# Spectral block and token/channel mixer on one core: where one weight tile is narrowed, and what the later stages' transfers and differences stand behind

## The chip, the cores and the metric

One core of one Trainium2 chip runs the whole program. The metric is the device time of one execution in microseconds (us); lower is better. TensorE (PE) does the matrix products, VectorE (DVE), ScalarE (ACT) and GpSimd (POOL) do the elementwise work, SyncE (SP) only issues transfers; ACT issues some as well. A queue name with a q (SPq, ACTq) is that engine's transfer issues.

## The reference, cut to what matters

```python
# x: (8, 3008, 256); w_r, w_i: (256, 256); w_tok1: (3008, 256); w_tok2: (256, 3008); w_ch1: (256, 1536); w_ch2: (1536, 256)
X = np.fft.rfft(x, axis=1)
Yr = Xr @ w_r - Xi @ w_i + b_r
Yi = Xr @ w_i + Xi @ w_r + b_i
Y  = soft_threshold(Yr, 0.01) + 1j * soft_threshold(Yi, 0.01)
x  = np.fft.irfft(Y, n=3008, axis=1)
h  = relu(x.T @ w_tok1) @ w_tok2      # over tokens
u  = x + h.T
return u + relu(u @ w_ch1) @ w_ch2    # over channels
```

The weights of the mixer arrive as 64-bit floats and are narrowed to 32 bits on the chip.

## The kernel before, in words

The transform over 3008 points is split as 47 x 64. Each product is made of three passes of a high and a low part (`mm3`, lines 223 to 225: high weight by high data, by low data, low weight by high data), so most operands exist as a pair: `xh`/`xl`, `hh`/`hlo`, `w2h`/`w2l`. The low part is made by `split`: ACT casts the high part (L158), DVE or POOL subtracts it (L161).

The eight batches are worked on in units, `UNITS = [[0], [1], [2, 3], [4, 5], [6, 7]]`. `begin` does unit 0 and the loads and narrowing of the weights. `spectral` is a generator for unit 1 and the three pairs. One of its steps `n` runs a forward product (`px`, L531), the complex mixing (`pm`), the inverse (`pi`) and the product with `w_tok1` (`gp`). Between them DVE makes `xtl` (L540) and `xs` (L541) out of `px`, and `z` (L576, L577: bias and sum; L583, L584: threshold) out of `pm`; POOL makes `yl` and some `xtl`. After the last step of a unit `gh` and `gl`, the relu of `gp`, are written to memory as `g_d` (L634 to L639).

The next units' first stage runs beside these steps as jobs (`beside`): `load` (x, from SP), `total` (the sum of the two halves of x on POOL, L277, and their difference on DVE, L278, both into `sd`), `divide` (`xh` on ACT, L673, and two `xl` on DVE, L676), `product` (`p`, L223 to L225, then `a` by ACT and a write of `a_d`). The table `when` says at which step a job is due; `sd` has one buffer.

Unit 0's channel mixing, in narrow chunks, is the other stream: `channel(n)` makes `u` (`pu`), then for each of twelve `f` a product `ph` with `w_ch1`, the pair `hh` (ACT, L1063) and `hlo` (DVE, L1064), and two steps later `po` with `w_ch2` (`second`). A loop at the end of the program takes steps of both streams in turn, by estimated times (the numbers that the generators yield). Behind the last narrow chunk `channel7`, the wide chunks of all other units, fills the rest of the span; it needs the weight sums that `weigh` and `weigh2` (L1159 to L1179) make in the last narrow chunk.

A scheduler gives each engine its order. `tc.issue_after(ins)` adds one rule to it: what is issued inside stands behind `ins` on `ins`'s own engine. Nothing waits for a semaphore because of it.

`w_ch2` comes in six tiles r0 to r5 of 128 x 512 values. Narrowing one takes two ACT passes (L187, L189) and six DVE passes (L192 to L197); `narrow_steps` (L168) gives the same work in two halves. Before, r0 and r1 are narrowed in `begin`, r2 to r5 in chunk 0 at `f` = 0, 2, 4, 6, and split one `f` later:

```python
                if f in late:
                    split_w2(*late.pop(f))
                if f % 2 == 0 and f // 2 + 2 < NF // 2:
                    late[f + 1] = f // 2 + 2, narrow_w2(f // 2 + 2)
```

Of the kernel before, what the change touches and what calls it, by code (L numbers as in the profile page):

```python
# [137 lines left out]
def tile_kernel(ctx: ExitStack, tc: tile.TileContext, io):  # L138
# [254 lines left out]
    def make_w(kp, aw, pool):  # L393
# [5 lines left out]
        wf = pool.tile([128, 2, DT], F32, name="wf", bufs=4) if kp < KP - 2 else wk.tile([128, 2, DT], F32, tag="xtl", name="wf", bufs=2)  # L399
# [63 lines left out]
    def narrow_w2(r, pool=None):  # L463
        return load_wide(io["moe_w_ch2"][r], 512, pool)
# [16 lines left out]
    def parts(u):  # L481
# [6 lines left out]
        def load_unit(g):  # L488
            src = io["x"][bs[0] // 2, g].rearrange("q i (b c) -> q i b c", b=2)
            if nb == 2:  # L490
                x = wc["wk2"].tile([120, 2, nb, C], F32, name="x", bufs=2)
            elif not plain:
# [8 lines left out]
            DMA.dma_start(out=x, in_=src[:, :, bs[0] % 2:bs[0] % 2 + nb])  # L501
# [116 lines left out]
        def close():  # L618
# [5 lines left out]
            elif u == len(UNITS) - 1:  # L624
                gs = [t4([128, 2, w], n) for n in ("gh", "gl")]
                gs = [[g.bitcast(F32R)[:, j] for j in range(2)] for g in gs]
            elif nb == 1:
                gs = [wc["wk2"].tile([128, CW], F32R, tag=n, name="g", bufs=3) for n in ("hh", "hlo")]
                gs = [[g[:, j * w:(j + 1) * w] for j in range(2)] for g in gs]
            else:  # L630
                gs = [[wc["wk2"].tile([128, CW], F32R, tag=n, name="g", bufs=3) for _ in range(2)] for n in ("hh", "hlo")]
# [54 lines left out]
    def spectral():  # L686
# [34 lines left out]
        for j in range(2):  # L721
            job("load", j)
        yield "wait"
        for q in range(2):
            load_ws(q)
        job("divide", 0)
# [5 lines left out]
        for n in range(len(flat) + LAG + 2):  # L732
# [22 lines left out]
            if 0 <= m < len(flat):  # L755
# [38 lines left out]
            if 0 <= m < len(flat) and kps[flat[m][0]][0] == 1:  # L794
# [4 lines left out]
                sts[o] = split_w(wf, G), split_e(ef, V)  # L799
# [797 lines left out]
```

## Time and profile before

| what | us |
|---|---|
| median of three runs | 2295.73 |
| the runs | 2295.45, 2301.96, 2295.73 |
| the profiled execution | 2295.41 |
| its span, first to last instruction | 2293.5 |
| TensorE busy in the span | 2266.3 |
| VectorE busy | 1709.5 |
| ScalarE busy | 1478.6 |
| GpSimd busy | 1372.4 |

1.9 us of the profiled execution's time lie outside its span. The mean granted TensorE clock is 0.999. The profile is one execution: a timeline row gives the start, the duration, engine, line, operation, what is written from what, and in brackets how long the engine had been idle and for whom. A row of waits gives the sum, the number and the longest of them.

### The profile page before, as it was taken

How to read it: one execution, taken by the hardware profiler on the slowest of the kernel's cores; microseconds unless marked ns; L12 is line 12 of the kernel's file. 1: busy time of each engine (PE TensorE's matmuls, PEld its weight loads, DVE VectorE, ACT ScalarE, POOL GpSimd, SP SyncE). 2: the span in 40 equal slices, each digit the busy share in tenths (PEclk: the TensorE clock that was granted, in tenths of full speed). 3: DMA queues.
4: the chain of work that ended last, by engine and by line, in shares of the span. 5: the costliest groups of instructions: out<-in, count | busy, mean ns of one | idle time of the engine just before them, and what ended most of it. 6: DMA issues, size and time to landing. Idle time of an engine off the chain costs nothing.

```text
span 2293.5 us, 34800 instructions
## 1 busy us (share of the span) xinstructions
PE 2266.3 (99%) x12095; PEld 1972.1 (86%) x12095; DVE 1709.5 (75%) x2801; ACT 1478.6 (64%) x2703; POOL 1372.4 (60%) x1111
## 2 busy tenths in 40 slices
PE   8999999999999999999999999999999999999999
PEld 7879999989989988888988888898888889888887
DVE  7976776687886767777777787777778776777877
ACT  6765555465654445776676777667677766667775
POOL 0000233354553321887787888778788877878886
PEclk9999999999999999999999999999999999999999
DMA  8885566787876443112222211222221122222101
GB/s 231 254 255 170 147 203 214 237 270 249 258 229 229 165 152 106 49 54 70 85 62 70 65 53 51 70 85 62 70 65 47 58 70 85 63 70 65 51 9 37
DMA packets 150957, 277.22 MB, mean 121 GB/s; under 512 B 11077, under 2 KB 95389, under 8 KB 150781
## 3 DMA queue, kind: packets, MB, share of 16 engines
q1 hardware_dynamic: 115106, 208.21, 30.2%
q10 hardware_dynamic: 35675, 66.78, 8.7%
q8 instruction: 96, 1.57, 0.3%
q14 instruction: 80, 0.66, 0.1%
HBM read 177.57 MB, written 97.39 MB: 120 GB/s over the span
## 4 chain that ended last, share of the span: by engine, by line
PE 87%; DVE 6%; DMA 3%; issue 2%; ACT 1%; SPq 1%; POOL 1%; ACTq 0%; POOLq 0%; DVEq 0%
PE l L134 15%; PE sx L134 14%; PE sz L134 11%; PE sy L134 10%; PE sw L134 7%; PE px L531 3%; PE pm L223 2%; PE pm L225 2%; PE pm L224 2%; PE gp L225 1%; PE gp L223 1%; PE gp L224 1%; PE po L224 1%; PE po L225 1%; PE po L223 1%
## 5 line engine op out<-in xcount | busy, mean ns | idle before, releaser
L1281 POOL TENSOR_TENSOR op<-ts,op 128x512 fp32r<-128x512 f32 (+2 forms) x500 | 634.7, 1291 | 271.3 <-ACT op L1314 267.7
L1314 ACT ACTIVATE op<-ts 128x512 fp32r<-128x512 f32 (+2 forms) x500 | 308.8, 619 | 62.1 <-DVE ts L1284 46.6
L1281 DVE TENSOR_TENSOR uf<-sy,uf 128x512 f32<-128x512 f32 (+2 forms) x229 | 154.4, 674 | 216.7 <-PE sy L134 216.2
L134 PE MATMUL l<-op,ws 128*128 128x512 f32 (+2 forms) x1125 | 311.8, 385 | 0.0
L134 PEld LDWEIGHTS l<-op,ws 128*128 128x128 f32 x1125 | 211.2, 188 | 39.8
L1310 ACT ACTIVATE x<-sx 128x512 f32<-128x512 f32 (+2 forms) x252 | 148.7, 590 | 137.5 <-PE sx L134 136.8
L134 PE MATMUL sx<-ub,w 128*128 128x512 f32 (+2 forms) x756 | 211.0, 387 | 0.4 <-DVE ts L1284 0.4
L134 PE MATMUL sx<-ub,ws 128*128 128x512 f32 (+2 forms) x756 | 209.8, 386 | 0.0
L161 POOL TENSOR_TENSOR yl<-z,yh 128x512 fp32r<-128x512 f32 x72 | 96.2, 1336 | 126.6 <-ACT yh L158 120.8
L134 PEld LDWEIGHTS sx<-ub,w 128*128 128x128 f32 x756 | 141.5, 188 | 29.5 <-DVE ts L1284 2.1
L134 PEld LDWEIGHTS sx<-ub,ws 128*128 128x128 f32 x756 | 141.8, 188 | 27.0
L1281 POOL TENSOR_TENSOR op<-b,op 128x512 fp32r<-128x512 f32 (+2 forms) x125 | 159.6, 1276 | 0.6 <-ACT op L1314 0.2
L1281 DVE TENSOR_TENSOR x<-sw,x 128x512 f32<-128x512 f32 (+2 forms) x126 | 85.7, 680 | 93.1 <-PE sw L134 92.9
L277 POOL TENSOR_TENSOR sd<-x 120x512 f32<-120x512 f32 x39 | 61.7, 1581 | 149.0 <-ACT hh L1063 45.0
L223 PE MATMUL pm<-wmh,xth 128*128 128x256 f32 x504 | 145.3, 288 | 2.0 <-DVE z L577 2.0
L1334 ACT ACTIVATE x<-x 128x512 f32<-128x512 f32 (+2 forms) x125 | 78.0, 624 | 107.3 <-DVE x L1281 107.3
L225 PE MATMUL pm<-wmh,xtl 128*128 128x256 f32 x504 | 142.5, 283 | 0.0
L224 PE MATMUL pm<-wml,xth 128*128 128x256 f32 x504 | 142.4, 283 | 0.0
L134 PE MATMUL sy<-op,w2h 128*128 128x512 f32 (+2 forms) x458 | 140.2, 387 | 0.3 <-DVE uf L1281 0.3
L161 POOL TENSOR_TENSOR xtl<-xs,xth 128x256 fp32r<-128x256 f32 x84 | 68.1, 811 | 104.9 <-ACT xth L158 66.7
L161 POOL TENSOR_TENSOR wt<-aw,wt 128x512 fp32r<-128x512 f32 x12 | 16.3, 1360 | 180.6 <-ACT wt L158 180.6
L134 PEld LDWEIGHTS sz<-g,b 96*128 96x128 f32 x836 | 106.8, 191 | 2.7
(240 smaller groups left out, 6616.3 us busy)
## 6 DMA issues: line engine op xcount, KB each, us to landing
wt<-wt_d SPq DMA_DIRECT2D x28, 940.0 KB, 5.6
x<-in_x SPq DMA_DIRECT2D x39, 480.0 KB, 6.1
a<-a_d SPq DMA_DIRECT2D x36, 512.0 KB, 6.1
wt<-ws_d SPq DMA_DIRECT2D x36, 512.0 KB, 5.1
b_d<-bt ACTq DMA_DIRECT2D x36, 512.0 KB, 5.6
a_d<-a ACTq DMA_DIRECT2D x36, 480.0 KB, 4.2
wt<-wt_d SPq DMA_DIRECT2D x21, 752.0 KB, 5.0
b<-b_d SPq DMA_DIRECT2D x32, 480.0 KB, 6.2
```

The costliest lines, as they stand in the source:

```text
L134: return lambda *args, **kw: self.tc.keep_in_program_order(op(*args, **kw))
L161: lo_eng.tensor_tensor(out=lo, in0=src, in1=hi.bitcast(F32), op=ALU.subtract)
L223: PE.matmul(out, lhsT=wh, rhs=xh, start=start, stop=False, skip_group_check=more)
L224: PE.matmul(out, lhsT=wh, rhs=xl, start=False, stop=False, skip_group_check=more)
L225: PE.matmul(out, lhsT=wl, rhs=xh, start=False, stop=stop, skip_group_check=more)
L277: eng.tensor_tensor(out=sd[:, 0], in0=x[:, 0], in1=x[:, 1], op=ALU.add)
L531: PE.matmul(pt[:, o:o + 128], lhsT=x, rhs=f2cols(2 * kp + ab), start=True, stop=True)
L1281: eng.tensor_tensor(out=out, in0=in0, in1=in1, op=op)
L1310: pins[key] = S.activation(out=t, in_=src, func=func)
L1314: pins[k] = S.activation(out=ops[k][:, 0], in_=v[k] if src is None else src, func=AF.Copy if k[0] == "t" else AF.Relu)
L1334: pins["x2r"] = S.activation(out=v["x2"], in_=v["x2"], func=AF.Relu)
```

## The change

- `w_ch2`: the raw words of r0, r1 and r2 are loaded at `n == NC + 7` of `begin`, all three are narrowed and split there. r3 and r4 are loaded at the end of `begin`, r5 at `f == 5` of chunk 0; they are narrowed in halves at `f` = 0, 1 and 2, 3 and 8, 9, each half behind that step's `hh` and `hlo`.
- The write of the first `w_tok2` tile moves in the code from `begin` to `f == 2` of chunk 0.
- Unit 1's x: every third tile has a buffer of its own (tag `xtl`), two of them are issued earlier on SP. The pairs' first x, the first `aw` and `ef` tiles stand behind the last x of unit 1 (`wc["loaded"]`).
- In `spectral`, the next job's `total` and `divide` are issued together, both behind the mixing's `summed` (L577 before) and the total behind `xs`; before, a later job's total came one step earlier. The next x is loaded behind a job's product.
- The `g_d` writes: unit 1 two instead of four, the low one on SP; of the first two pairs the low parts on SP; the last pair two instead of four. `weigh` and `weigh2` stand behind `hlo`.

```diff
+    def steps_w2(r):
+        raw = load_raw(io["moe_w_ch2"][r], 512)
+        yield
+        tmp = wk.tile([128, 2, 512], F32, tag="o", name="wide", bufs=3)
+        steps = narrow_steps(raw, tmp[:, 0], tmp[:, 1])
+        next(steps)
+        yield
+        next(steps)
+        split_w2(r, tmp[:, 0])
+        yield
...
+            elif not plain and g % 3 == 0:
+                x = wk.tile([120, 2, nb, C], F32, tag="xtl", name="x", bufs=2)
...
-            DMA.dma_start(out=x, in_=src[:, :, bs[0] % 2:bs[0] % 2 + nb])
+            wc["loaded"] = DMA.dma_start(out=x, in_=src[:, :, bs[0] % 2:bs[0] % 2 + nb])
...
             if u:
-                for i in range(2):
-                    for j in range(2):
-                        PUT.dma_start(out=g_d[u][i, :, j * w:(j + 1) * w], in_=gs[i][j].bitcast(F32))
+                if nb == 1 or u == len(UNITS) - 1:
+                    gs = [[g] for g in whole]
+                for i, g in enumerate(gs):
+                    n = 2 * w // len(g)
+                    for j, part in enumerate(g):
+                        (DMA if i and u < len(UNITS) - 1 else PUT).dma_start(out=g_d[u][i, :, j * n:(j + 1) * n], in_=part.bitcast(F32))
...
-        for j in range(2):
-            job("load", j)
+        with tc.issue_after(wc["loaded"].ins):
+            for j in range(2):
+                job("load", j)
         yield "wait"
...
+        yield "rest"
+        with tc.issue_after(wc["hh"].ins), tc.issue_after(wc["hlo"].ins):
+            job("divide", 0)
...
+                ahead = when.get(n + 1)
+                with tc.issue_after(summed.ins), tc.issue_after(wc["xs"].ins):
+                    if ahead is not None:
+                        job("total", ahead)
                 with tc.issue_after(summed.ins):
-                    for ahead, what in ((when.get(n + 1), "divide"), (when.get(n + 2), "total")):
-                        if ahead is not None and jobs[ahead][0] > 2 and (what == "divide" or ahead > NG):
-                            job(what, ahead)
+                    if ahead is not None and jobs[ahead][0] > 2:
+                        job("divide", ahead)
...
-            ahead = when.get(n + 1)
-            if ahead is not None and jobs[ahead][0] > 2:
-                job("load", ahead + 2)
-            if j is not None and jobs[j][0] == 2:
+            if j is not None:
                 job("load", j + 2)
...
+                if n == NC + 7:
+                    f = [load_raw(io["moe_w_ch2"][r], 512, early) for r in range(3)]
                 if n == NC + 8:
                     split_wt2(0)
-                    keep_wt2(0)
+                    wc["wt2_0"] = wts[0]
                     done += extra(1)
-                if n in (NC + 9, NC + 10):
-                    f.append(narrow_w2(len(f), early))
+                if n in (NC + 9, NC + 10, NC + 11):
+                    f[n - NC - 9] = load_wide(None, 512, raw=f[n - NC - 9])
...
-        for r in range(2):
+        for r in range(3):
             split_w2(r, f[r])
+        for r in (3, 4):
+            w2s[r] = steps_w2(r)
+            next(w2s[r])
...
-                if f in late:
-                    split_w2(*late.pop(f))
-                if f % 2 == 0 and f // 2 + 2 < NF // 2:
-                    late[f + 1] = f // 2 + 2, narrow_w2(f // 2 + 2)
+                if f == 5:
+                    w2s[5] = steps_w2(5)
+                    next(w2s[5])
+                with tc.issue_after(wc["hh"].ins), tc.issue_after(wc["hlo"].ins):
+                    if f in (0, 1, 2, 3, 8, 9):
+                        next(w2s[{0: 3, 1: 3, 2: 4, 3: 4}.get(f, 5)])
...
                 if seven and f in SUMS:
-                    (weigh2 if SUMS.index(f) % 2 else weigh)(SUMS.index(f) // 2)
+                    with tc.issue_after(wc["hlo"].ins):
+                        (weigh2 if SUMS.index(f) % 2 else weigh)(SUMS.index(f) // 2)
```

What this does to the engines' orders is shown at three places (numbers behind a name tell its buffers apart). The first is DVE at the end of `begin`, where unit 1's third x tile is divided (its `xl` is made from `sd_1284` before, `sd_1294` now) and r2 is narrowed (`raw_1419` into `wide_1421` before, `raw_1148` into `wide_1237` now). Before:

```order
L161 TENSOR_TENSOR xl_1288<-sd_1275,xh_1287 120x512
L277 TENSOR_TENSOR sd_1313<-x_1282 120x256
L278 TENSOR_TENSOR sd_1313<-x_1282 120x256
L161 TENSOR_TENSOR et_2677<-ef_2144,et_2677 128x256
L193 TENSOR_SCALAR wide_1421<-raw_1419 128x512
L192 TENSOR_SCALAR wide_1421<-wide_1421 128x512
L194 SCALAR_TENSOR_TENSOR wide_1421<-wide_1421 128x512
L195 TENSOR_SCALAR wide_1421<-wide_1421 128x512
L161 TENSOR_TENSOR w2l_1331<-wide_1188,w2h_1330 128x512
L161 TENSOR_TENSOR xl_1317<-sd_1284,xh_1316 120x512
L161 TENSOR_TENSOR w2l_1331<-wide_1214,w2h_1330 128x512
L635 SCALAR_TENSOR_TENSOR gl_1306<-gp_1018,gh_1305 128x256
```

Now:

```order
L196 TENSOR_TENSOR wide_1237<-raw_1148,wide_1237 128x512
L277 TENSOR_TENSOR sd_1294<-x_1174 120x256
L197 TENSOR_TENSOR wide_1237<-wide_1237 128x512
L278 TENSOR_TENSOR sd_1294<-x_1174 120x256
L161 TENSOR_TENSOR xl_1298<-sd_1285,xh_1297 120x512
L277 TENSOR_TENSOR sd_1323<-x_1292 120x256
L278 TENSOR_TENSOR sd_1323<-x_1292 120x256
L161 TENSOR_TENSOR xl_1327<-sd_1294,xh_1326 120x512
L277 TENSOR_TENSOR sd_1344<-x_1321 120x256
L278 TENSOR_TENSOR sd_1344<-x_1321 120x256
L161 TENSOR_TENSOR w2l_1341<-wide_1191,w2h_1340 128x512
L645 SCALAR_TENSOR_TENSOR gl_1316<-gp_1018,gh_1315 128x256
```

r2's last pass (L197) now stands ahead of the second tile's `xl`, and the third tile's `xl` ahead of the first `w2l`; before, it stood behind four passes over r2 and a `w2l`.

The second is ACT at the end of unit 1, where `g` is written out (L639, now L652) while the first steps of the pairs run. Before:

```order
L538 COPY xs_4669<-px_4664 128x256
L639 DMA g_d1_95<-g_4648 128x256
L634 ACTIVATE g_4648<-gp_2990 128x256
L639 DMA g_d1_95<-g_4649 128x256
...
L539 CAST xth_4670<-px_4664 128x512
L673 CAST xh_4704<-sd_4609 120x1024
```

Now:

```order
L548 COPY xs_4664<-px_4659 128x256
L549 CAST xth_4665<-px_4659 128x512
L644 ACTIVATE g_4643<-gp_3010 128x256
L612 COPY bt_4708<-pi_4709 128x512
L652 DMA g_d1_95<-g_4643 128x512
L612 COPY bt_4708<-pi_4714 128x512
L158 CAST xth_4665<-xs_4664 128x256
```

`xth` stood behind four writes of `g` (the last two are left out) and stands ahead of the one that is left on ACT.

The third is DVE in the pairs, where a job's difference (`sd`, L278) and its two `xl` (L676, now L689) are made. Before, from one job's difference to its two `xl` in the next step:

```order
L278 TENSOR_TENSOR sd_4983<-x_4861 120x512
L583 TENSOR_SCALAR z_4976<-z_4976 128x512
L584 TENSOR_TENSOR z_4976<-z_4976 128x512
L540 TENSOR_TENSOR xtl_5017<-px_5010,xth_5016 128x512
L541 TENSOR_TENSOR xs_5015<-px_5010,xs_5015 128x256
L576 TENSOR_TENSOR z_5061<-pm_5042,bias_80 128x512
L577 TENSOR_TENSOR z_5061<-pm_5042,z_5061 128x512
L676 TENSOR_TENSOR xl_5070<-sd_4983,xh_5068 120x512
L583 TENSOR_SCALAR z_5061<-z_5061 128x512
L676 TENSOR_TENSOR xl_5071<-sd_4983,xh_5068 120x512
L584 TENSOR_TENSOR z_5061<-z_5061 128x512
L540 TENSOR_TENSOR xtl_5085<-px_5078,xth_5084 128x512
```

Now, the same of one job:

```order
L587 TENSOR_TENSOR z_5526<-pm_5507,z_5526 128x512
L278 TENSOR_TENSOR sd_5533<-x_5354 120x512
L593 TENSOR_SCALAR z_5526<-z_5526 128x512
L594 TENSOR_TENSOR z_5526<-z_5526 128x512
L550 TENSOR_TENSOR xtl_5561<-px_5554,xth_5560 128x512
L689 TENSOR_TENSOR xl_5538<-sd_5533,xh_5536 120x512
L689 TENSOR_TENSOR xl_5539<-sd_5533,xh_5536 120x512
L551 TENSOR_TENSOR xs_5559<-px_5554,xs_5559 128x256
```

The difference and the two `xl` of a job were a step apart, or the difference of the next job stood behind the `xl`, right ahead of `xtl`; now a job's three passes all stand between one step's `z` and the next `xs`. Of the order at the end of the narrow chunk one thing is used further on: on TensorE the 22 matmuls of the next `pu` and six of `ph` now stand ahead of the `po` that reads the third `hlo`; before, they stood behind it.

## Rows read from the trace of the kernel before

**Rows 1.** The page: the span, and TensorE's busy time.

```profile
span 2293.5 us, 34800 instructions
PE 2266.3 (99%) x12095; PEld 1972.1 (86%) x12095; DVE 1709.5 (75%) x2801; ACT 1478.6 (64%) x2703; POOL 1372.4 (60%) x1111
```

**Rows 2.** Busy time of each engine in the stretch that the change touches (columns: stretch, its length, busy us and count of PE, PEld, DVE, ACT, POOL, granted TensorE clock, share of the transfer engines, GB/s), the first and fourth of five stretches from 140 to 860 us, and their sum.

```profile
140.00:300.00 160.00, 156.02 (x927) 148.10 (x926) 118.08 (x213) 85.95 (x165) 23.20 (x18) 0.99 0.60 179
...
580.00:700.00 120.00, 118.45 (x767) 106.90 (x767) 99.94 (x159) 71.17 (x138) 61.72 (x51) 1.00 0.77 239
sum 720.00, PE 710.49 PEld 652.47 DVE 523.51 ACT 381.08 POOL 255.60; mean PE 142.10 PEld 130.49 DVE 104.70 ACT 76.22 POOL 51.12
```

**Rows 3.** What TensorE waited for between 140 and 900 us (sum, number of waits, longest).

```profile
PE po L224 <- DVE hlo L1064: 2.9, 4, 1.2
PE pm L223 <- DVE z L577: 2.0, 3, 1.0
PE p L223 <- DVE xs L541: 2.0, 2, 1.1
PE p L224 <- DVE xl L161: 1.5, 1, 1.5
PE pi L223 <- DVE xs L541: 0.9, 2, 0.4
PE p L223 <- ACT xh L158: 0.8, 1, 0.8
PE ph L223 <- DVE xs L541: 0.5, 1, 0.5
```

**Rows 4.** The chain of waits between 135 and 160 us (start, us, what): its two longest pieces of `w_ch2`.

```profile
134.45 6.61 DMA raw<-in_moe_w_ch
...
150.05 6.57 DMA raw<-in_moe_w_ch
```

**Rows 5.** DVE's timeline around the first of them: r2's first pass, and the `xl` behind the narrowing; then the pass over the next tile and the `hlo` behind it.

```profile
141.08 0.43 DVE L193 TENSOR_SCALAR wide<-raw 128x512 uint32<-128x512 uint32 x1 [4.07 <-DMA raw<-in_moe_w_ch]
...
143.93 0.68 DVE L161 TENSOR_TENSOR xl<-sd,xh 120x512 fp32r<-120x512 f32 x1
...
156.65 0.43 DVE L193 TENSOR_SCALAR wide<-raw 128x512 uint32<-128x512 uint32 x1 [2.45 <-DMA raw<-in_moe_w_ch]
156.99 1.20 DVE L1064 SCALAR_TENSOR_TENSOR hlo<-ph,hh 128x470 fp32r<-128x470 f32 x2
```

**Rows 6.** The same columns as rows 2, in stretches of 2 us behind the first stall; the granted clock is the third number from the end.

```profile
144.00:146.00 2.00, 1.33 (x8) 1.25 (x9) 2.00 (x6) 0.42 (x2) 0.00 (x0) 0.91 1.03 248
146.00:148.00 2.00, 2.00 (x7) 1.70 (x6) 1.56 (x4) 1.10 (x2) 0.29 (x1) 0.50 0.97 316
148.00:150.00 2.00, 2.00 (x14) 1.92 (x13) 2.00 (x4) 0.07 (x1) 1.41 (x1) 0.74 1.03 370
```

**Rows 7.** ACT's timeline at the end of unit 1: the writes of `g_d`, and the `xth` behind them.

```profile
454.24 0.78 ACTq L639 DMA_DIRECT2D g_d<-g  x1
...
455.09 3.11 ACTq L639 DMA_DIRECT2D g_d<-g  x3
458.24 0.59 ACT L539 CAST xth<-px 128x512 fp32r<-128x512 f32 x1 [2.79 <-DMA a_d<-a]
```

**Rows 8.** Transfers issued between 452 and 463 us: the four writes of `g_d` (size of one, median us from issue to landing).

```profile
g_d<-g ACTq DMA_DIRECT2D x4, 128.0 KB, 7.9
```

**Rows 9.** TensorE's timeline: the single stalls of rows 3 that the sum speaks of.

```profile
157.69 0.48 PE L224 MATMUL po<-hlo,w2h 128*128 128x470 f32 x1 [1.02 <-DVE hlo L1064]
...
441.22 0.47 PE L223 MATMUL p<-xh,f1r 120*128 120x512 f32 x1 [0.85 <-DVE xs L541]
...
460.09 0.47 PE L223 MATMUL p<-xh,f1r 120*128 120x512 f32 x1 [1.12 <-DVE xs L541]
461.41 0.36 PE L223 MATMUL pm<-wmh,xth 128*128 128x256 f32 x1 [0.85 <-DVE z L577]
...
506.98 0.47 PE L223 MATMUL pi<-yh,et 128*128 128x512 f32 x1 [0.45 <-DVE xs L541]
...
681.15 0.36 PE L223 MATMUL pm<-wmh,xth 128*128 128x256 f32 x1 [0.96 <-DVE z L577]
...
861.33 0.48 PE L224 MATMUL po<-hlo,w2h 128*128 128x470 f32 x1 [1.17 <-DVE hlo L1064]
```

**Rows 10.** DVE's timeline ahead of four of them: a difference ahead of 441, the first of eight that took 1.7 us and more between 421 and 686 us; a difference ahead of 507; the last of the eight and a weight sum ahead of 681; the `hlo` ahead of 861.

```profile
435.45 1.78 DVE L278 TENSOR_TENSOR sd<-x 120x512 f32<-120x512 f32 x1
...
504.12 1.78 DVE L278 TENSOR_TENSOR sd<-x 120x512 f32<-120x512 f32 x1
...
675.64 1.79 DVE L278 TENSOR_TENSOR sd<-x 120x512 f32<-120x512 f32 x1
...
678.28 1.39 DVE L1159 TENSOR_TENSOR a<-w 128x1024 f32<-128x1024 f32 x1
...
860.63 0.64 DVE L1064 SCALAR_TENSOR_TENSOR hlo<-ph,hh 128x470 fp32r<-128x470 f32 x1
```

**Rows 11.** All differences (L278) between 300 and 840 us: their number, the shortest, median and longest in ns.

```profile
L278 DVE TENSOR_TENSOR sd<-x x31: 678/798/1786, 311.1 to 685.3; 120x512 f32<-120x512 f32 x31
```

**Rows 12.** POOL's timeline: the sum that ran beside the difference of 435.45.

```profile
435.20 1.47 POOL L277 TENSOR_TENSOR sd<-x 120x512 f32<-120x512 f32 x1
```

**Rows 13.** What TensorE waited for ahead of 140 us: the one wait on narrowed weights of the first 64-bit matrix.

```profile
PE p L302 <- DVE wide L197: 0.6, 1, 0.6
```

More of the change, by code (lines that the diff above doesn't have):

```diff
@@ L398, in make_w @@
                 PE.matmul(pt[ab * 64:(ab + 1) * 64, i], lhsT=wc["fw"][:, i, j0:j0 + 64], rhs=aw[:, ab], start=True, stop=True)
-        wf = pool.tile([128, 2, DT], F32, name="wf", bufs=4) if kp < KP - 2 else wk.tile([128, 2, DT], F32, tag="xtl", name="wf", bufs=2)
+        wf = pool.tile([128, 2, DT], F32, name="wf", bufs=4) if kp < KP - 2 else wk.tile([128, 2, DT], F32, tag="xth", name="wf", bufs=2)
         for i in range(2):
@@ L624, in close @@
             elif u == len(UNITS) - 1:
-                gs = [t4([128, 2, w], n) for n in ("gh", "gl")]
-                gs = [[g.bitcast(F32R)[:, j] for j in range(2)] for g in gs]
+                whole = [t4([128, 2, w], n).rearrange("p j w -> p (j w)").bitcast(F32R) for n in ("gh", "gl")]
+                gs = [[g[:, j * w:(j + 1) * w] for j in range(2)] for g in whole]
             elif nb == 1:
-                gs = [wc["wk2"].tile([128, CW], F32R, tag=n, name="g", bufs=3) for n in ("hh", "hlo")]
-                gs = [[g[:, j * w:(j + 1) * w] for j in range(2)] for g in gs]
+                whole = [wc["wk2"].tile([128, CW], F32R, tag=n, name="g", bufs=3) for n in ("hh", "hlo")]
+                gs = [[g[:, j * w:(j + 1) * w] for j in range(2)] for g in whole]
             else:
@@ L719, in close @@
                 parts_of(kps[q][0]).close()
-        for j in range(2):
-            job("load", j)
+        with tc.issue_after(wc["loaded"].ins):
+            for j in range(2):
+                job("load", j)
         yield "wait"
-        for q in range(2):
-            load_ws(q)
-        job("divide", 0)
+        with tc.issue_after(wc["loaded"].ins):
+            for q in range(2):
+                load_ws(q)
+        yield "rest"
+        with tc.issue_after(wc["hh"].ins), tc.issue_after(wc["hlo"].ins):
+            job("divide", 0)
         job("load", 2)
@@ L798, in spectral @@
                     keep_split(o - 1, *sts[o - 1])
-                sts[o] = split_w(wf, G), split_e(ef, V)
+                with tc.issue_after(wc["hh"].ins):
+                    sts[o] = split_w(wf, G), split_e(ef, V)
                 if kps[o + 2][0] == 1:
@@ L815, in begin @@
         pieces = [(q, t) for q in range(3) for t in range(2)]
[L816 removed]
+        aws, wfs1, wide, done = {}, {}, {}, 0.0
         def transform(k):
@@ L949, in tile_kernel @@
     assert done_g == len(groups)
-    wts, wfs, b2s, ufs, us, late, mixed = {}, {}, {}, {}, {}, {}, {}
+    wts, wfs, b2s, ufs, us, late, mixed, w2s = {}, {}, {}, {}, {}, {}, {}, {}
     def load_wt2(g, pool=None, parts=(0, 1)):
@@ L973, in steps_wt2, with keep_wt2 @@
         return narrow_steps(raw, tmp[:, 0], tmp[:, 1])
-    def keep_wt2(g):
+    def keep_wt2(g, w=None):
         u, _, s, k = groups[g]
         if u == 0:
-            DMA.dma_start(out=wt2_d[:, :, s * TOKS:(s + k) * TOKS], in_=wts[g][:, :, :k * TOKS].bitcast(F32))
+            w = wts[g] if w is None else w
+            DMA.dma_start(out=wt2_d[:, :, s * TOKS:(s + k) * TOKS], in_=w[:, :, :k * TOKS].bitcast(F32))
     def split_wt2(g, parts=(0, 1)):
```

7 lines of the change are left out of this document (3 added, 4 removed).

## The prediction, before any run of the changed kernel

> **What bounds the kernel now.** I read the page first. TensorE is busy 2266.3 us of a span of 2293.5 [rows 1]: 27.2 us of idle time are all that a change of order can return, beside any time at the lower clock. The change touches what runs before 880 us; behind that TensorE's order is the same in both. So I asked for the busy time by stretch. From 140 to 860 us TensorE is busy 710.49 of 720 us [rows 2]: 9.5 us idle, 4.0 of them between 140 and 300. One more wait, 1.17 us, lies at 861 [rows 9]. Then I asked what TensorE waited for: by `hlo` 2.9 us in four waits, by `z` 2.0, by `xs` 2.0, 0.9 and 0.5, by `xl` 1.5, by `xh` 0.8 [rows 3], 10.6 us in all. Every one of them is a product that came late from DVE or ACT, while DVE as a whole has room: 99.94 of 120 us in its fullest stretch [rows 2]. So the order on DVE and ACT is what costs, not the sum of their work.
>
> The chain of waits tells why the first two stalls occur: the raw words of two tiles of `w_ch2`, issued at 134.45 and 150.05, take 6.61 and 6.57 us [rows 4]. DVE stands 4.07 us for the first, 2.45 for the second, and the `xl` and `hlo` that TensorE needs are queued behind [rows 5]. After the first stall the granted clock is 0.91, 0.50 and 0.74 of full speed in three stretches of 2 us [rows 6]; 0.50 is the lower level, 1.2 GHz, full speed is 2.4 GHz.
>
> **The change, part by part.** The sum is against the profiled execution, 2295.41 us, which is the span and 1.9 us around it; the median of the runs, 2295.73, is 0.3 us above it.
>
> A, r2 narrowed earlier. The two stalls are 0.8 and 1.5 us [rows 3]. The clock costs (0.09 + 0.50 + 0.26) x 2 = 1.7 us [rows 6]. Together 4.0. In the new order r2's raw words follow those of r0 and r1, and its last DVE pass is ahead of the second `xl`. The six passes that come in ahead need some 3 x 0.43 + 3 x 0.68 = 3.3 us, and the 4.07 us for which DVE stood [rows 5] cover them; without that cover `xl` would come 3.3 us later. What is late next is `gl`: one `w2l` stands ahead of its first half, a `w2l` and an `xl` ahead of its second, each 0.68 [rows 5]. SP's order also puts the raw words of r4 ahead of the `b` that `pu` needs; r4 waits for the third x tile's difference, an event some 3 us later than before, while `b` waits for a product that does not move. I take 0.4 us for what this leaves, between 0 and the 4.0 of the stall itself: gain 3.6.
>
> B, the `hlo` ahead of the narrowing. Three of the four `hlo` waits, 2.9 - 1.17 = 1.7 us [rows 3, 9], are in chunk 0 and the next: 1.02 at 157.69, the others shorter. The halves of r3 to r5 now stand behind `hh` and `hlo` of their step, and their raw words are asked for earlier. The work is the same, six DVE passes a tile; it is hidden as before. Gain 1.7, at least the 1.0.
>
> C, the writes of `g_d`. ACT issues four of them, 0.78 and 3.11 us, and `xth` starts 2.79 us late behind [rows 7]; TensorE waits 1.12 and 0.85 us at 460 [rows 9]. In the new order `xth` is ahead of the only write left on ACT; the other goes to SP, which has no engine behind it that waits so soon. Gain 2.0. The third `z` wait, 2.0 - 0.85 - 0.96 = 0.2 [rows 3, 9], is at the end of a pair behind the same kind of writes, two of which leave ACT: gain 0.2. The Trainium skill says that the engine which issues a transfer only saves its sequencer's time, "usually small relative to the DMA itself" (DMA: Bandwidth & Descriptors, section Issuing engines are not separate DMA queues). Here the issues took 3.9 us against 7.9 to landing [rows 7, 8], and it is ACT's time, not the transfer's, that `xth` waited for. By that sentence the sum would lose its 2.2 us of C; I go by the rows.
>
> D, a weight sum. 1.39 us of `weigh` run at 678.28, in the middle of the pairs [rows 10], and TensorE waits 0.96 [rows 9]. Behind `hlo` of its own chunk it moves to the end. Gain 1.0.
>
> E, the end of the narrow chunks. The third `hlo` starts at 860.63, behind passes of the weight sums [rows 10], and TensorE waits 1.17 [rows 9]. DVE's order there is worse now, by one weight sum as long as the 1.39 us of D, but TensorE has 28 other matmuls to do first: at a mean of 118.45 / 767 = 0.15 us [rows 2] these are 4.3 us, against 1.17 + 1.39. Gain 1.2, at worst none.
>
> F, the pairs. The waits by `xs` at 441.22 (0.85), the two of `pi` (0.9) and the one of `ph` (0.5) [rows 3, 9] are 2.25 us. Ahead of the two of which I show the DVE rows stands a difference of 1.78 us [rows 10]; the shortest takes 0.678 and the median is 0.798 [rows 11], so the long ones are stretched by 1.1 us, with POOL's sum beside them [rows 12]. In the new order no difference stands right ahead of `xtl`, which removes these waits. But now all three passes of a job stand between `z` and `xs`, 3 x 0.68 = 2.0 us, in each of the 31 jobs that rows 11 count. No row shows that in every job, so I bound it. A difference of 1.78 us in that place cost 0.45 where it cost most by itself [rows 9, 10]: 31 x 0.45 = 14.0 us above, and nothing below, since some steps hold two `xl` and a difference already. I take 0.11 each, the two `pi` waits spread over the eight stretched differences from 435.45 to 675.64 [rows 10], since in most of these eight places the delay cost nothing: 3.4 us. Net loss 1.15.
>
> G, the start. Two x tiles of unit 1 stand ahead of two tiles of `w_tok1` on SP. The nearest wait on narrowed `w_tok1` is 0.6 us [rows 13]; I take half, loss 0.3, between 0 and 0.6. The moved write of `w_tok2` costs nothing: on SP it stands between the same transfers as before.
>
> Sum: 3.6 + 1.7 + 2.2 + 1.0 + 1.2 - 1.15 - 0.3 = 8.25 us. 2295.41 - 8.25 = **2287.2 us**. 0.3%, 6.9 us, is about what a measurement of this kernel can tell from no change: 2288.5 is the bound against the profiled execution.
>
> **The rivals.**
> 1. The pairs give more back. If each job costs 0.25 us, 7.8 in place of 3.4, the time is 2291.6; for it speaks that DVE's load is high there [rows 2], against it that some steps held all three passes before. No change. Chance 0.24.
> 2. The change does not do what it says at the start: `b` comes late behind r4's raw words, `pu` waits as `p` did, and the clock falls again. A's 3.6 are gone: 2290.8. For it speaks that a raw tile took 6.6 us to land [rows 4]; against it that the pairs' x no longer compete there. No change. Chance 0.10.
> 3. Slower: DVE's three passes of a job meet POOL. A difference beside POOL's sum was stretched by 1.1 us [rows 10 to 12], and an `xl` also reads two tiles as a difference does. If all three are stretched in ten of the 31 jobs, about the third in which a difference is stretched now, `xs` comes 3.3 us later there; less the 0.65 us of slack that a stretched one leaves (1.1 late, 0.45 waited), that is 2.65 x 10 = 27 us; if one of the three is stretched in each job, 0.45 x 31 = 14. I price it in between, at 0.7 a job: without F's loss the gains are 11.65, and 2295.41 - 11.65 + 21.7 = 2305.5. It decides from 11.65 / 31 = 0.38 us a job on. Against it: POOL's sum still runs as soon as `sd` is free, while the difference now waits for the step, so these two should meet less often. Chance 0.12. The Trainium skill would have it so whenever both run: VectorE with two inputs from SBUF and a reading GpSimd take turns, and whichever starts first holds the other off for the whole instruction (SBUF — State Buffer, section Who interferes with whom). The stretched differences agree, 1.78 for 0.68.
> 4. C is not returned, since other work on ACT is as late: 2289.4, no change. Chance 0.04.
>
> **How the numbers follow.** The forecast has 0.50. The chance of faster by over 0.3% is that of the forecast, 0.50; within 0.3% are rivals 1, 2 and 4, 0.38; slower 0.12. The range begins at 2283.0, where every wait from 140 us on (10.6) and the clock's 1.7 come back, and ends at 2299.0: that takes in rivals 1, 2 and 4 with their bounds and the mild end of rival 3.
>
> **What would show it.** Right: no wait of `p` between 140 and 146 us and full clock to 152; `hlo` without a DMA wait ahead of it at 156; `xth` at the end of unit 1 directly behind `xs`; no weight sum before 840 us; TensorE busy over 717 of 720 us from 140 to 860. Wrong: a wait of `pu` on `b` with a clock of 0.5 near 145 (rival 2); many waits of `pm`, `p` or `pi` on `xs` or `z` between 300 and 700 us (rival 1), with `xl` and differences of 1.2 us and more (rival 3); the wait of `po` at 861 back as one of `ph`.

## The result: slower by 0.6%, and the profile after

| | before | changed |
|---|---|---|
| median (five runs each, on one chip), us | 2295.85 | 2312.98 |
| lowest and highest run of the changed kernel, us | | 2310.67, 2313.97 |
| ratio to before | | 1.0062 [1.0047, 1.0076] |
| profiled execution, us | 2295.41 | 2310.67 |
| its span, us | 2293.5 | 2308.8 |

Ratios, here and below, compare the runs as a whole and are not the quotients of the medians (here 1.0075). Predicted were 2287.2 us and a range of 2283.0 to 2299.0. The time lies outside the range, on the other side of no change. The page of the changed kernel answers to [rows 1]:

```profile
span 2308.8 us, 34754 instructions
PE 2275.2 (99%) x12095; PEld 1969.5 (85%) x12095; DVE 1725.2 (75%) x2801; ACT 1479.5 (64%) x2703; POOL 1370.5 (59%) x1111
```

Busy TensorE rose by 8.9 us with the same 12095 matmuls and a full clock. In the profile a matmul of 512 columns lasts 0.39 us, and the next one may start 0.23 us behind it (three of `gp` start at 611.71, 611.93 and 612.16), so the first 0.16 us of a stall pass as busy: the stall of `p` at 617.76, shown further down, cost 1.11 us and 0.96 of them count as idle. So busy time is a poor measure of what was lost, and I count matmuls too. What TensorE waited for between 140 and 900 us, to be read against [rows 3] (sum, number, longest):

```profile
PE p L224 <- DVE xl L689: 3.9, 7, 1.0
PE pu L223 <- ACT wt L158: 2.6, 2, 1.5
PE p L223 <- DVE xs L551: 1.6, 2, 1.1
PE p L223 <- ACT xh L686: 1.6, 3, 0.7
PE ph L223 <- ACT a L304: 1.2, 1, 1.2
PE gp L223 <- DVE g L645: 0.9, 1, 0.9
...
PE pm L223 <- DVE z L587: 0.7, 2, 0.5
...
PE p L223 <- DVE hlo L1088: 0.3, 1, 0.3
```

The waits by `hlo`, all but 0.3 us, and by `z`, all but 0.7, are gone as forecast. Of those by `xs`, 1.6 us are left, and in their place stand `xl` and `xh` of the pairs' first-stage product `p`, and `wt`. The stretches of the changed kernel (columns as in [rows 2]):

```profile
140.00:260.00 120.00, 120.00 (x707) 114.20 (x706) 83.85 (x160) 64.90 (x125) 10.68 (x8) 1.00 0.57 168
260.00:440.00 180.00, 175.14 (x1085) 160.93 (x1084) 125.57 (x187) 91.55 (x174) 60.13 (x46) 1.00 0.67 210
440.00:700.00 260.00, 249.68 (x1578) 218.45 (x1578) 209.03 (x319) 143.86 (x277) 122.26 (x105) 1.00 0.78 241
```

and of the kernel before:

```profile
140.00:260.00 120.00, 116.02 (x671) 109.45 (x670) 87.27 (x162) 64.56 (x124) 10.50 (x8) 0.99 0.64 191
260.00:440.00 180.00, 179.50 (x1126) 168.10 (x1124) 122.38 (x191) 93.17 (x178) 57.18 (x46) 1.00 0.64 200
440.00:700.00 260.00, 255.19 (x1658) 230.54 (x1657) 207.64 (x336) 150.48 (x292) 131.25 (x109) 1.00 0.79 247
```

The first stretch now has no idle time and 36 matmuls more. The second has 41 fewer, the third 80 fewer. For a closer account I took the time from each matmul's start to the next and summed by how much it differs from the median of that shape of matmul in the kernel before; shorter times count against longer ones. This is **lost time** in the text below, in us. Time at the lower clock is in it: 1.7 of the 7.8 us of the kernel before, and of e8's 1.7 from 140 to 260 and 3.4 in the pairs.

| stretch, us | before | changed | e1 | e4 | e8 | e14 |
|---|---|---|---|---|---|---|
| 0 to 140 | 39.5 | 40.0 | 40.7 | 41.5 | 41.1 | 41.6 |
| 140 to 260 | 7.8 | 1.9 | 2.2 | 2.8 | 9.1 | 3.6 |
| 260 to 440 | 1.8 | 7.5 | 5.6 | 6.4 | 1.7 | 1.8 |
| 440 to 700 | 6.9 | 20.2 | 4.1 | 5.0 | 22.4 | 3.3 |
| 700 to 880 | 3.7 | 3.4 | 2.6 | 2.6 | 4.5 | 2.5 |
| 880 to the end | 12.6 | 14.7 | 13.8 | 12.8 | 14.0 | 13.8 |
| sum | 72.3 | 87.6 | 68.9 | 71.0 | 92.9 | 66.6 |

The sums of the first two differ by 15.3 us, as their spans do. The changed kernel gains 6.0 us from 140 to 260 and loses 5.7 in the next stretch and 13.3 in the pairs. (e1 to e14 are the experiments below.)

**One job of the pairs.** DVE in the changed kernel (start, us, what):

```profile
612.71 1.05 DVE L278 TENSOR_TENSOR sd<-x 120x512 f32<-120x512 f32 x1
...
614.74 0.68 DVE L550 TENSOR_TENSOR xtl<-px,xth 128x512 fp32r<-128x512 f32 x1
615.34 2.37 DVE L689 TENSOR_TENSOR xl<-sd,xh 120x512 fp32r<-120x512 f32 x2
617.63 0.41 DVE L551 TENSOR_TENSOR xs<-px,xs 128x256 f32<-128x256 f32 x1
```

ACT, POOL and TensorE beside it:

```profile
613.79 1.05 ACT L686 CAST xh<-sd 120x1024 fp32r<-120x1024 f32 x1 [0.91 <-DVE sd L278]
...
615.55 1.60 POOL L161 TENSOR_TENSOR yl<-z,yh 128x512 fp32r<-128x512 f32 x1 [2.34 <-ACT yh L158]
...
617.76 0.50 PE L224 MATMUL p<-xl,f1r 120*128 120x512 f32 x1 [0.96 <-DVE xl L689]
```

The difference, `xh`, the two `xl` and the `p` that reads them are now one chain. The second `xl` ends at 617.71 and `p` starts 0.05 us later, after 0.96 us of idle time. The job at the same place before: DVE, then TensorE's last `p` with `xl`.

```profile
608.15 0.68 DVE L278 TENSOR_TENSOR sd<-x 120x512 f32<-120x512 f32 x1
...
614.03 0.68 DVE L676 TENSOR_TENSOR xl<-sd,xh 120x512 fp32r<-120x512 f32 x1
...
618.19 0.39 PE L224 MATMUL p<-xl,f1r 120*128 120x512 f32 x1
```

The second `xl` was done at 614.71, 3.48 us ahead of its reader. Over the 23 jobs whose difference lies between 440 and 700 us that lead had a median of 2.0 us and a least value of 1.3; now the median is 0.06 and 13 of the 23 have no more. And from the rows of `xl` in that stretch (ns: shortest, median, longest; below them who waited, us and times), before and changed:

```profile
L676 DVE TENSOR_TENSOR xl<-sd,xh x48: 677/682/1165, 442.4 to 694.3; 120x512 fp32r<-120x512 f32 x48
...
who waited for it (us, times):
  POOL sd L277: 1.6, 1
```

```profile
L689 DVE TENSOR_TENSOR xl<-sd,xh x46: 675/686/1792, 446.0 to 697.0; 120x512 fp32r<-120x512 f32 x46
...
who waited for it (us, times):
  PEld p L224: 10.3, 18
  PE p L224: 3.9, 7
```

TensorE waited for no `xl` of the pairs before. Now its weight loads waited 18 times for one and its matmuls seven times.

### The profile page after: what moved, and what is told of

Same layout as the page of the kernel before. It is cut to its first block, busy times and chain, and to the rows that moved or that the text cites. A ratio compares the mean times of both kernels' runs of the same rounds, so it can differ in the third digit from the quotient of the medians.

```text
span 2308.8 us, 34754 instructions
## 1 busy us (share of the span) xinstructions
PE 2275.2 (99%) x12095; PEld 1969.5 (85%) x12095; DVE 1725.2 (75%) x2801; ACT 1479.5 (64%) x2703; POOL 1370.5 (59%) x1111
## 4 chain that ended last, share of the span: by engine, by line
PE 82%; DVE 10%; issue 2%; DMA 2%; ACT 2%; POOL 1%; SPq 1%; ACTq 0%; DVEq 0%; POOLq 0%
PE l L134 14%; PE sx L134 13%; PE sz L134 10%; PE sy L134 10%; PE sw L134 7%; PE px L541 2%; PE pm L223 2%; PE pm L225 2%; PE pm L224 2%; PE gp L224 1%; PE gp L225 1%; PE gp L223 1%; PE ph L223 1%; PE po L223 1%; PE po L225 1%
## 5 line engine op out<-in xcount | busy, mean ns | idle before, releaser
L277 POOL TENSOR_TENSOR sd<-x 120x512 f32<-120x512 f32 x39 | 52.2, 1338 | 261.1 <-DMA aw<-w_d 155.5
L1310 DVE TENSOR_TENSOR x<-sw,x 128x512 f32<-128x512 f32 (+2 forms) x126 | 85.7, 680 | 92.9 <-PE sw L134 92.9
L134 PE MATMUL sw<-ub,ws 128*128 128x512 f32 (+2 forms) x378 | 107.6, 393 | 1.7 <-DVE op L1313 1.3
```

Source lines behind the costliest of these rows:

```text
L134: return lambda *args, **kw: self.tc.keep_in_program_order(op(*args, **kw))
L277: eng.tensor_tensor(out=sd[:, 0], in0=x[:, 0], in1=x[:, 1], op=ALU.add)
L1310: eng.tensor_tensor(out=out, in0=in0, in1=in1, op=op)
```

## The experiments

My theory: the total one step later (F) costs the pairs 13 us (20.2 for 6.9 in the table) and the start another 8, while A to E are returned. The rivals: the late load of x does it, or DVE's load by itself. Each ratio is to runs of the kernel before made beside it; e4, e8, e11 and e13 ran on another chip than the other experiments.

**e1, the order of the jobs put back in the changed kernel**, all else kept.

```diff
-                ahead = when.get(n + 1)
-                with tc.issue_after(summed.ins), tc.issue_after(wc["xs"].ins):
-                    if ahead is not None:
-                        job("total", ahead)
                 with tc.issue_after(summed.ins):
-                    if ahead is not None and jobs[ahead][0] > 2:
-                        job("divide", ahead)
+                    for ahead, what in ((when.get(n + 1), "divide"), (when.get(n + 2), "total")):
+                        if ahead is not None and jobs[ahead][0] > 2 and (what == "divide" or ahead > NG):
+                            job(what, ahead)
...
-            if j is not None:
+            ahead = when.get(n + 1)
+            if ahead is not None and jobs[ahead][0] > 2:
+                job("load", ahead + 2)
+            if j is not None and jobs[j][0] == 2:
                 job("load", j + 2)
```

> The changed kernel, with only the jobs' order put back: the next job's total a step ahead of its divide, the next x loaded a step earlier. Against the profile of before, the changed kernel loses 13 us between 440 and 700 us (pairs) and 8 us between 260 and 420 us (chunks of unit 0 beside unit 1). Theory (in the pairs a job's difference, its xh, its two xl and its product p now all fall into one step, so p comes late): the 13 us come back, 2298 to 2302 us, and no wait of p on xl or xh is left behind 440 us. Rival (the loss of the pairs comes from the writes of g_d on SP or the later loads): 2308 us or more, the waits stay.

Median 2291.55, ratio 0.9985 [0.9976, 0.9994]: 21 us back by the medians and 18 by the ratios, more than the theory gave. Every wait of `p` on `xl` or `xh` in the pairs is gone and the median lead is 2.0 us again. Of the lost time 18.7 us are back in the profiled execution, 16.1 of them in the pairs; the medians differ by 2.7 more, since the profile of the changed kernel is its fastest run and that of e1 one above its median. What TensorE waits for there:

```profile
PE pi L223 <- DVE xs L551: 0.9, 2, 0.4
PE pi L223 <- ACT a L304: 0.3, 1, 0.3
PE p L223 <- DVE xs L551: 0.2, 1, 0.2
```

**e8, that order alone, in the kernel before** (the same lines the other way, nothing else).

> The kernel before, with only the jobs' order of the change (total and divide of a job in one step, the next x behind the product). Theory (this part alone makes the loss; putting it back returned 21 us): 2312 to 2318 us, with waits of p on xl and xh between 440 and 700 us. Rival (it costs only together with the later transfers and splits): below 2305 us.

Median 2311.44, ratio 1.0062 [1.0049, 1.0076]: this part alone makes the whole loss. Lost time in the pairs is 22.4 us, 19.0 without the lower clock, for 20.2 in the changed kernel, and the waits by `xl` are there:

```profile
PE p L224 <- DVE xl L676: 4.7, 8, 0.9
PE px L531 <- ACT a L304: 2.7, 1, 2.7
PE p L223 <- ACT xh L673: 1.6, 3, 0.7
...
```

**e4, the total a step earlier again, x still loaded late.** It tells the two halves of the edit apart.

```diff
-                ahead = when.get(n + 1)
+                ahead, later = when.get(n + 1), when.get(n + 2)
...
                 with tc.issue_after(summed.ins), tc.issue_after(wc["xs"].ins):
-                    if ahead is not None:
-                        job("total", ahead)
+                    if later is not None and jobs[later][0] > 2 and later > NG:
+                        job("total", later)
```

> The changed kernel, with a job's total a step ahead of its divide again, but the next x still loaded behind the product, as in the change. Theory (the difference that comes only in the step of its product is what costs): 2290 to 2294 us, as with the whole job order put back. Rival (the later load of x costs): 2303 us or more, with waits of L277 or L278 on the transfer of x.

Median 2291.77, ratio 0.9979 [0.9970, 0.9988], lead 2.0 us, lost time 5.0 in the pairs. The step of the total is the cause; the late load costs nothing that can be seen.

**e6, the pairs' product a step later in the changed kernel**, which gives `xl` its lead back from the other end.

```diff
-            if j is not None:
+            done_j = when.get(n - 1)
+            if j is not None and jobs[j][0] == 2:
                 job("product", j)
-                yield 3.5 if jobs[j][0] == 2 else 1.4
+                yield 3.5
+            if done_j is not None and jobs[done_j][0] > 2:
+                job("product", done_j)
+                yield 1.4
```

> The changed kernel with only the pairs' product p one step later; DVE's and POOL's orders stay those of the changed kernel. Theory (latency: difference, xh, xl and p in one step): the waits of p on xl and xh, 5.5 us between 140 and 900 us, are gone and the time falls by 4 to 9 us, to 2304 to 2309 us. Rival (DVE's passes are stretched by POOL beside them, whoever waits): the waits move to pm, pi and gp, 2311 to 2315 us.

Median 2305.85, ratio 1.0038 [1.0020, 1.0056]. No `p` of the pairs waits for `xl` or `xh` any more, so the lead is what those waits were. The median lies in the range expected for this run, but seven us are won, not 16, and other waits stand in their place:

```profile
PE pm L223 <- DVE z L587: 6.8, 3, 2.6
PE pi L223 <- ACT a L304: 4.9, 2, 3.5
...
```

DVE ahead of the two longest of the waits by `z`, which end at 483.8 and 697.8 us:

```profile
479.01 2.40 DVE L689 TENSOR_TENSOR xl<-sd,xh 120x512 fp32r<-120x512 f32 x2 [2.83 <-ACT xh L686]
...
692.98 2.40 DVE L689 TENSOR_TENSOR xl<-sd,xh 120x512 fp32r<-120x512 f32 x2 [3.06 <-ACT xh L686]
```

DVE stood some 3 us for `xh`, then the two `xl` took 2.40 beside a `yl`, and `xtl`, `xs` and `z` were queued behind them: the late passes also hold up what stands behind them on DVE, as F and rival 1 had it. Why `a` comes late I did not settle. This profile, 2313.15 us, is one of the slowest of nine runs that spread from 2298.59 to 2313.61, with mean granted clocks from 1.000 in the fastest to 0.995 in the slowest three. In it the clock is 0.97 of full speed from 260 to 440 us and 0.98 from 440 to 700, which costs 5.1 and 5.7 us; 20.2 us are lost in the pairs, as in the changed kernel. So the seven us are the median of runs with and without time at the lower clock; the fastest run stands 14.4 us below the median of the changed kernel, whose profile had the full clock. How much of the loss the lead alone makes, e6 does not tell.

**e13, the pairs' difference on POOL in the changed kernel.** It takes one of the three passes off DVE.

```diff
-        V.tensor_tensor(out=sd[:, 1], in0=x[:, 0], in1=x[:, 1], op=ALU.subtract)
+        (V if pool is not None or w <= C else eng).tensor_tensor(out=sd[:, 1], in0=x[:, 0], in1=x[:, 1], op=ALU.subtract)
```

> The changed kernel with the pairs' and unit 2's differences made by POOL instead of DVE; nothing else is changed, so total and divide stay in one step of the code. POOL makes sum and difference as soon as sd is free, so xh no longer waits for a DVE pass of its own step. Theory (the late difference, then xh, then xl make p late): the waits of p on xl and xh go, 2293 to 2300 us. Rival (DVE's passes are stretched by POOL beside them): POOL reads 1.3 to 1.8 us more in each job, so the stretching grows and the time stays at 2308 us or more.

Median 2324.01, ratio 1.0119 [1.0105, 1.0132], the slowest of all, and a miss. In the pairs `p` waits for no `xl` and no `xh`; TensorE waits for `a` and `yl`. I take it that these stand behind a longer chain on ACT and POOL, but did not follow it:

```profile
PE px L541 <- ACT a L304: 8.1, 10, 1.4
PE pi L223 <- ACT a L304: 4.2, 1, 4.2
PE pi L224 <- POOL yl L161: 2.9, 2, 1.4
...
```

DVE had 34 us less to do than in the changed kernel (1690.8 for 1725.2) and the kernel was 11 us slower, 5.1 of them time at the lower clock in the pairs of this profile. So less work on DVE alone did not bring the time back; e1, e8 and e4 put the loss on the step of the total.

**e2, the start put back in the changed kernel:** the pairs' x, `aw` and `ef` no longer behind unit 1's last x, their splits and the first divide no longer behind `hh` and `hlo`.

```diff
-        with tc.issue_after(wc["loaded"].ins):
-            for j in range(2):
-                job("load", j)
+        for j in range(2):
+            job("load", j)
         yield "wait"
-        with tc.issue_after(wc["loaded"].ins):
-            for q in range(2):
-                load_ws(q)
-        yield "rest"
-        with tc.issue_after(wc["hh"].ins), tc.issue_after(wc["hlo"].ins):
-            job("divide", 0)
+        for q in range(2):
+            load_ws(q)
+        job("divide", 0)
...
-                with tc.issue_after(wc["hh"].ins):
-                    sts[o] = split_w(wf, G), split_e(ef, V)
+                sts[o] = split_w(wf, G), split_e(ef, V)
```

> The changed kernel, with only the transfers behind unit 1's last x and the splits behind hh put back to where they were (pairs' x, aw and ef of unit 1, divide of the first job). Theory: the 8 us between 260 and 420 us come from unit 1's aw and ef being split on DVE and POOL in the middle of the chunks; they come back, 2303 to 2307 us, and the waits of pu on ACT's wt at 287 and 348 us are gone. Rival (these waits come from the new halves of the narrowing or the job's order): 2310 us or more. A gain of the start (r2 narrowed earlier, full clock at 146 us) may be lost again, up to 5 us: then 2308 to 2312 us with the stretch from 260 on as before.

Median 2307.01, ratio 1.0045 [1.0032, 1.0058]. Lost time from 260 to 440 falls from 7.5 to 1.9 us, as the theory has it, while the pairs keep 19.5. A stall by `ul` stands at 152 us:

```profile
PE ph L224 <- DVE ul L1044: 1.4, 1, 1.4
```

**e3, both put back** (e1 and e2 together).

> The changed kernel with both put back: what is left is w_ch2's third tile ahead of the chunk and the halves, the x tag of unit 1, the writes of g_d and the weight sums behind hlo. Theory (two separate losses, the rest of the change gains): 2288 to 2292 us, below the kernel before by 4 to 8 us. Rival (the rest is worth nothing): 2295 us or more.

Median 2290.27, ratio 0.9975 [0.9966, 0.9984], as expected.

**e11, e1 with only the splits freed** (`split_w` and `split_e` no longer behind `hh`, the last hunk of e2).

> The changed kernel with the jobs' order put back and unit 1's weights split without standing behind hh; the transfers stay behind unit 1's last x. With the jobs' order alone put back, 4.9 us more than before are lost between 260 and 300 us, where pu waits for ACT's wt. Theory (the splits behind hh cost that): 2286 to 2289 us. Rival (the late transfers of aw and ef cost it): 2290 to 2293 us, the waits stay.

Median 2296.22, ratio 0.9997 [0.9988, 1.0005]: a miss. In the code it stands between e1 and e3; by its ratio it is slower than e3, while its interval and that of e1 overlap. The span of its profile, 2291.2 us, is hardly longer than that of e1, 2290.6, but that profile is the fastest of its eleven runs; its lost time is 3.6 us more from 140 to 260, by `hlo` and `wt`, and 1.6 less in the next stretch. What made the median stays open.

**e14, e1 with only the pairs' x left behind unit 1's last x** (all other lines of e2's edit undone).

```diff
         with tc.issue_after(wc["loaded"].ins):
             for j in range(2):
                 job("load", j)
         yield "wait"
-        with tc.issue_after(wc["loaded"].ins):
-            for q in range(2):
-                load_ws(q)
-        yield "rest"
-        with tc.issue_after(wc["hh"].ins), tc.issue_after(wc["hlo"].ins):
-            job("divide", 0)
+        for q in range(2):
+            load_ws(q)
+        job("divide", 0)
...
-                with tc.issue_after(wc["hh"].ins):
-                    sts[o] = split_w(wf, G), split_e(ef, V)
+                sts[o] = split_w(wf, G), split_e(ef, V)
```

> The changed kernel with the jobs' order put back, and of the later transfers only the pairs' first x behind unit 1's last x; unit 1's aw and ef are loaded and split where they were before. With jobs and all transfers put back, 2.3 us more than in the change are lost between 140 and 160 us; with the jobs alone put back, 4.9 us more than before between 260 and 300. Theory (the pairs' x is what competes at 140 us, the late aw and ef what costs at 280): both go, 2285 to 2288 us. Rival (aw and ef compete at 140 too): 2289 to 2292 us.

Median 2288.83, ratio 0.9963 [0.9951, 0.9976]: 8.5 us faster than before by the ratio and 7.2 by the medians, the best of all, just outside what was expected. This is the change without what cost it the time. What TensorE waited for between 140 and 900 us is all of this:

```profile
PE pi L223 <- DVE xs L551: 0.9, 2, 0.4
PE po L224 <- DVE hlo L1084: 0.9, 2, 0.6
PE p L223 <- DVE xs L551: 0.9, 1, 0.9
PE ph L223 <- DVE xs L551: 0.4, 1, 0.4
PE pi L224 <- POOL yl L161: 0.4, 1, 0.4
```

**e15, the `w_ch2` part alone in the kernel before** (`steps_w2`, the loads and halves of r2 to r5 and the first `w_tok2` write as the change has them; the `g_d` writes, the weight sums, the jobs, the x buffer and the start as before).

> The kernel before, with only w_ch2's new narrowing (r0 to r2 ahead of the chunk, r3 to r5 in halves; the write of w_tok2's first tile with it). The prediction's terms A and B are 3.6 and 1.7 us: 2290 to 2291 us, the waits of p at 143 to 145 and of po at 157 us gone and the clock full at 146. Rival (the pairs' x and the raw words still share the transfers at 140 us, so something else waits there): 2293 us or more.

Median 2295.66, ratio 0.9994 [0.9985, 1.0003]: a miss, no change. The stall of `p` at 143 is gone, but TensorE now stops for `ul` instead, 1.39 us at 149.65:

```profile
146.00:148.00 2.00, 2.00 (x19) 1.88 (x17) 1.76 (x2) 1.36 (x4) 1.56 (x1) 1.00 1.06 384
148.00:150.00 2.00, 0.61 (x4) 0.32 (x3) 2.00 (x5) 2.00 (x5) 0.08 (x1) 1.00 0.98 390
```

In e14, with the pairs' x out of the way (and the other parts of the change in place), the same two stretches are full:

```profile
146.00:148.00 2.00, 2.00 (x16) 1.79 (x14) 2.00 (x5) 1.19 (x3) 0.00 (x0) 1.00 1.07 296
148.00:150.00 2.00, 2.00 (x15) 1.85 (x14) 1.99 (x5) 1.00 (x2) 0.00 (x0) 1.00 0.91 310
```

**e16, the `g_d` writes and the weight sums alone in the kernel before** (C, D and E).

```diff
+                if nb == 1 or u == len(UNITS) - 1:
+                    gs = [[g] for g in whole]
+                for i, g in enumerate(gs):
+                    n = 2 * w // len(g)
+                    for j, part in enumerate(g):
+                        (DMA if i and u < len(UNITS) - 1 else PUT).dma_start(out=g_d[u][i, :, j * n:(j + 1) * n], in_=part.bitcast(F32))
...
                 if seven and f in SUMS:
-                    (weigh2 if SUMS.index(f) % 2 else weigh)(SUMS.index(f) // 2)
+                    with tc.issue_after(wc["hlo"].ins):
+                        (weigh2 if SUMS.index(f) % 2 else weigh)(SUMS.index(f) // 2)
```

> The kernel before, with only the writes of g_d changed and the weight sums behind hlo. The prediction's terms C, D and E are 2.2, 1.0 and 1.2 us: 2291 to 2292 us, and no wait at 460, 681 and 861 us. Rival, the Trainium skill's sentence that the issuing engine saves little (DMA: Bandwidth & Descriptors, section Issuing engines are not separate DMA queues): C is not returned, 2293 to 2294 us with the wait at 460 as before.

Median 2293.37, ratio 0.9984 [0.9976, 0.9993]: 3.7 us by the ratio, 2.7 by the medians, where the prediction had 2.2 + 1.0 + 1.2 = 4.4. The median lies in the range of the run's rival, but not its sign, the wait at 460 as before. At the end of unit 1 `xth` no longer stands behind writes:

```profile
456.78 0.60 ACT L539 CAST xth<-px 128x512 fp32r<-128x512 f32 x1
...
457.70 0.33 ACTq L642 DMA_DIRECT2D g_d<-g  x1
458.86 0.41 ACT L158 CAST xth<-xs 128x256 fp32r<-128x256 f32 x1 [0.26 <-DVE xs L541]
```

TensorE's waits of 1.12 and 0.85 us there [rows 9] are gone, and so are those at 681 and 861. So rival 4 is out, and the sentence of the Trainium skill that the issuer's time is "usually small relative to the DMA itself" (DMA: Bandwidth & Descriptors, section Issuing engines are not separate DMA queues) does not hold for this place, where the writes held ACT for 3.9 us against 7.9 to landing [rows 7, 8]. Of the 3.9 us, 3.1 are the four issues themselves. The last of them began at 457.34, behind the landing of a write of `a_d` at 457.26, which is what the bracket behind `xth` in rows 7 names.

## Why the prediction was wrong, point by point

**The step that failed is F.** It asked which product would come late from DVE and took `xs`, the next pass on DVE behind the three. It costed the delay of `xs` by the two waits of `pi` there had been, spread over eight stretched differences: 0.11 us a job. The reader of the moved passes themselves, `p`, was not looked at, so its wait stood in the sum at nothing. The order shown ahead of the prediction had the sign of it: on DVE the difference and its second `xl` came from nine places apart to five, in one step instead of two, with ACT's `xh` between them. Their lead over `p` could have been read from the trace of before: least 1.3 us, median 2.0, in a chain from the difference's end to the second `xl`'s end of 6.4 us, of which 3.3 is left now. What was paid is (20.2 - 4.1) / 23 = 0.70 us a job from 440 to 700, by the lost time of the changed kernel less that of e1, against 0.11.

**Rival 3** ended on the right side, but that its price of 0.7 a job is what was measured is luck: it priced `xs`, over 31 jobs, and what came late for `p` were `xl` and `xh`. Its slowing beside POOL did occur: from 440 to 700 us 16 `xl` took over 0.9 us. Eleven of them, up to 1.79, started while POOL was at a `yl`, and five, up to 1.23, while it was at an `xtl`; before, six did, up to 1.17, all at an `xtl`. Right behind such a one lie 14 of the 15 stalls of `p` by `xl`, 6.1 of 6.3 us of lost time. The other 6.2 us are at the `p` that reads `xh`, in 30 small pieces. The Trainium skill's rule that VectorE with two SBUF inputs and a reading GpSimd hold each other off (SBUF — State Buffer, section Who interferes with whom) agrees: in the job shown two `xl` took 2.37 us beside a `yl`, where two of 0.68 would be 1.36. The first started ahead of `yl` and was not slowed; the second started at 615.94, when 1.21 us of `yl` were left, and took 1.77. The argument against the rival, that POOL's sum and the difference would meet less often, was true of the sum (mean 1628 ns before, 1297 after) and beside the point: `xl` met `yl`, and the difference met `xtl` (eight of 23 took over 0.9 us beside one, for three before). How the 16 us divide between the lost lead and the slowing isn't shown, and some 4 of them are not at `p`; against a lead of 1.3 us and more the 1.1 us of a slow `xl` would have cost nothing, as the six before cost nothing. **Rival 1**, more waits by `xs` and `z`, did not occur: between 300 and 700 us one by `xs` (1.15) and two short ones by `z` are left.

**A and B** came back in kind: full clock and no idle time from 140 to 260, 6.0 us of lost time less, for 3.6 + 1.7. But the `w_ch2` part alone, in e15, brought 1.4 us, which its interval does not tell from nothing: `ul` is late next. The stretch where it stopped is full in e14, with the pairs' x behind unit 1's last x. e3 differs from e14 by that transfer alone and has the stall by `ul`, 1.49 us at 154; e14 has none. What it is worth in all the runs do not tell (2290.27 and 2288.83, intervals that overlap). The prediction named `gl` and `b` as next late and used the x order only as an argument against rival 2. Rival 2 did not occur.

**C, D, E** were right: 3.7 us in e16 for 4.4. In the changed kernel C was half hidden: a wait of `gp` for `g`, 0.95 us, stands at 458.61 instead. e3 has the same wait with the jobs put back, so the jobs alone did not bring it.

**G** was mis-sized, and its main part left out. It costed two x tiles, but not that the first `aw` and `ef` now load behind them and their splits wait for `hh`. Lost time from 260 to 440 rose by 5.7 us with TensorE waiting for `wt` and `a`; e2 takes it back, and so does e14, which keeps the two x tiles. So the loads, the splits and the first divide make it; which of these, e11 does not tell.

Without F and G the terms add up to 3.6 + 1.7 + 2.2 + 1.0 + 1.2 = 9.7 us; e14, which is the change without F and without most of G, gained 8.5 [5.5, 11.3], worked out from its ratio. The sum came close, but in part by luck: of the 5.3 of A and B their own part brought 1.4 alone (e15), and e14 also moves the pairs' x, for which the sum had no term. What the pairs would lose was not forecast.

## What to carry to other kernels

When a pass is moved later, read from the trace how long its product lay ready before its reader started, for every reader, and above all for the product of the same job; compare the least lead with the delay, and only then ask who is queued behind it. A list of what matmuls waited for does not hold all stalls: by `xl` it had seven, and 18 stood at weight loads. Count matmuls in a stretch, or sum the distance from start to start. Undo a mixed change in parts, since here parts that gain some 8 us stood beside one that costs about 20.

## What the runs showed of the hardware that I had not expected

A TensorE that waits can look busier: the changed kernel lost 15.3 us of span and TensorE's busy time rose by 8.9. How much a DVE subtraction of 120 x 512 values is slowed by POOL went with what was left of the POOL pass it met. In the profiles of before, the changed kernel, e1, e4, e6 and e8 there are 279 `xl` and 138 differences of the pairs between 440 and 700 us. Each that started while a POOL pass was under way took what was left of that pass and 0.55 us, but not less than 0.68; each that started first, or with POOL idle, took 0.67 to 0.69. All agree within 0.03 us but one, which started 0.01 us behind a `yl` and took 0.68. A step's delay changed which pass was met and how early in it. Moving the difference to POOL took 34 us of work from DVE, added 51 to POOL's busy time and made the kernel slower by 11 us: 1.29 us each there, median, against 1.05 on DVE in the changed kernel.
